# One weight load of 128 rows cut into loads of 112, 8 and 8 rows, in a decode kernel for one core

## The chip, the core and the metric

The kernel runs on one core of a Trainium2 chip. A core has five engines with queues of their own: TensorE (PE, with its weight loads shown as PEld), VectorE (DVE), ScalarE (ACT), GpSimd (POOL) and SyncE (SP), and sixteen DMA engines that move data between the chip's memory (HBM) and the core's on-chip memory (SBUF, 128 partitions). The metric is the device time of one execution, in microseconds (us).

## The reference

One step of decoding for two sequences (B = 2). Two branches take the same input x and are mixed by a gate:

```python
def reference(A_x, A_k_cache, A_v_cache, A_wq, A_wo, B_x, B_w1, B_w2, B_w3, B_w4, gate_w):
    x = A_x                                                   # [2, 1, 1024]
    g = sigmoid((x * gate_w).sum(-1, keepdims=True))
    # branch A: attention of 32 heads over a cache of 16384 positions, 128 numbers each
    q = (x @ wq).reshape(B, 1, 32, 128).transpose(0, 2, 1, 3)
    p = softmax(einsum("bhqd,bhkd->bhqk", q, k_cache) * 128 ** -0.5)
    a = einsum("bhqk,bhkd->bhqd", p, v_cache) ... @ wo
    # branch B: a mixer and an MLP
    h = gelu(layernorm(x) @ w1)
    hs = shifted_groups(h) @ w2          # each quarter of h shifted along the one position
    x1 = x + hs
    b = x1 + gelu(layernorm(x1) @ w3) @ w4      # w2: [1024, 1024], w3: [1024, 3584], w4: [3584, 1024]
    return g * a + (1 - g) * b
```

All inputs are bfloat16. With one position the four shifted groups are all zeros, so the operand of w2 is zero and hs is zero; the kernel does the product with w2 all the same, with an operand of zeros.

## The kernel before, in words

All large data passes through one buffer in SBUF, `ring`, of five slots; a slot has 32 KB in each of the 128 partitions. Every large load is one DMA issued by SP, and each partition receives one contiguous row of it. The loads come in one fixed order: the first eighth of w3, wq, w2, the rest of w3, w4, then for each of 32 pairs of heads the K cache and the V cache (two heads, two slots, 64 KB in each partition), and last wo in two halves, the second half cut into six DMAs of falling size.

The order and the waits are planned in Python before anything is emitted. `queue_load` appends a load with its slots, and `pump` (lines 306 to 317) issues the next loads as long as their slots are free; a load waits for the instruction that last read its slots. `release` gives slots back and calls `pump`. `arrived(key)` is the event on which a reader of the data waits: the semaphore of the load's last DMA and its value. Each DMA adds 16 to its semaphore, and the plan counts up by 16 for each. A load of one DMA uses the semaphore of its first slot, `s_ring`; a load of several, before, uses one semaphore for each, `s_tail`.

The slots are fixed by these lines:

```python
w_slots = {"wq": (0, 1), "w2": (2,), "w3": (3, 4), "w4": (0, 1)}
k_slots = ((2, 3), (3, 4))
```

V goes to slots 0 and 1. So wq, w2 and w3 wait for nothing, w4 waits for the matmuls with wq (L604), the first K load waits for the matmuls with w2 (L509) and for the part of w3's (L476) that reads slot 3, and each later K or V load waits for the matmuls of the pair before (L652 for K, L688 for V).

`runs` (L329) builds the DMA of a weight matrix: partition p gets rows p·r to p·r + r - 1 of the matrix in one run. For w2 that is eight rows of 1024 numbers, 16 KB in each of 128 partitions. Before, w2 is one such DMA.

In the prologue the core computes q with wq (L604), the gate (L404 to L417), the product with w2 (L509, `row_stage`), its columns (L543, L549), a layer norm, the product with w3 (L476, `dense_stage`), gelu, and the product with w4 (L509 again). Then the pairs run in a loop: DVE transposes K in place (L646), PE makes the scores (L652), a softmax over DVE, PE and ACT follows, PE multiplies with V (L688), and the result of a pair is kept. At the end come the product with wo (L727), two copies to `orow` (L756) and four small stores of the output.

ACT issues, at the start, six small loads: x and the gate weights to `xg_row`, and x in four parts to `xrow`, two rows each; and at the end two of the four stores.

## Time and profile before

| | us |
|---|---|
| median of 3 runs | 1322.31 |
| lowest run | 1322.17 |
| time of the profiled execution | 1322.18 |
| its span, first to last instruction | 1320.9 |
| PE busy in it | 786.0 (60%) |
| DVE busy in it | 659.8 (50%) |

The mean granted TensorE clock in the profiled execution is 0.794 of full speed. DMA moved 570.60 MB at a mean of 432 GB/s.

In the lines of the profile, "tile<-source" names what an instruction writes and reads, L and a number is the line of the kernel, and x and a number is how many instructions a row stands for. The slices cut the span into forty equal parts, 33.0 us each; their digits are tenths. DMA share is the mean busy share of the sixteen DMA engines. The row of a queue gives packets, megabytes and the share of the sixteen engines' span. The row of a DMA issue gives the size in KB and the time from issue to landing. The chain of waits is followed back from the last instruction; each piece has its start, its length and what ran. In a short window a DMA share can come out over 1, since packets are counted as a whole.

### The profile page before, as it was taken

To read this page: it belongs to the slowest core of one execution; us is meant where nothing else is said; L and a number is where in the kernel's file an instruction comes from. 1 tells how busy PE (TensorE), PEld (TensorE's weight loads), DVE (VectorE), ACT (ScalarE), POOL (GpSimd) and SP (SyncE) were. 2 spreads that over 40 slices of the span, in tenths; PEclk is the share of its full clock that TensorE was granted. 3 is DMA by queue.
4 is the path that set the end of the run, shared out by engine and by line. 5 is a ranking of instruction groups with operands and counts; after the bars stand their busy time and mean duration, and the time that the engine had idled before them with its cause. 6 is when DMAs were issued, how large, how long until landed. Compare 5 with 4: busy or idle time off the path is not lost.

```text
span 1320.9 us, 12282 instructions
## 1 busy us (share of the span) xinstructions
PE 786.0 (60%) x5235; PEld 335.0 (25%) x5235; DVE 659.8 (50%) x527; ACT 45.7 (3%) x99; POOL 19.6 (1%) x78
## 2 busy tenths in 40 slices
PE   1645467655546666555666655566565556756457
PEld 1622222222222222222222222222222222222223
DVE  0254446655444665544466554446655445665444
ACT  0000000000000000000000000000000000000000
POOL 3000000000000000000000000000000000000000
PEclk9976888877688877777887777788777778887778
DMA  9999999999999999999999999999999999999998
GB/s 414 433 427 441 431 431 443 431 429 443 431 429 443 431 431 441 431 433 441 429 435 439 429 435 439 431 435 437 431 435 437 431 437 435 431 439 433 431 439 370
DMA packets 11121, 570.60 MB, mean 432 GB/s; under 512 B 1235, under 2 KB 1763, under 8 KB 2022
## 3 DMA queue, kind: packets, MB, share of 16 engines
q1 hardware_dynamic: 11080, 570.43, 99.7%
q8 instruction: 8, 0.13, 0.0%
q14 instruction: 3, 0.02, 0.0%
q10 hardware_dynamic: 30, 0.01, 0.0%
HBM read 570.44 MB, written 0.00 MB: 432 GB/s over the span
## 4 chain that ended last, share of the span: by engine, by line
DMA 69%; PE 24%; DVE 6%; issue 1%; SPq 0%; POOL 0%
DMA ring<-in_A_k_cache_dram 65%; PE ps L652 22%; DVE ring L646 6%; DMA ring<-in_A_wo_dram 2%; DMA ring<-in_A_wq_dram 2%; PE ps L476 1%; PE ps L604 1%; DVE hsd L543 0%; PE ps L509 0%; PE ps L400 0%; SPq L333 0%; DVE orow L756 0%; POOL mv L441 0%; PE ps L727 0%; DVE q_f L616 0%
## 5 line engine op out<-in xcount | busy, mean ns | idle before, releaser
L652 PE MATMUL ps<-ring,Z 128*128 128x512 bf16 x2048 | 531.5, 417 | 382.3 <-DVE ring L646 381.4
L646 DVE STREAM_TRANSPOSE ring<-ring 128x2048 f32<-128x2048 f32 x256 | 565.2, 2275 | 268.2 <-DMA ring<-in_A_k_cache_dram 268.2
L652 PEld LDWEIGHTS ps<-ring,Z 128*128 128x128 bf16 x2048 | 202.3, 104 | 698.7 <-issue 457.2
L688 PE MATMUL ps<-ring,PT_sb 128*32 128x512 bf16 x2048 | 172.8, 512 | 4.2 <-DVE recip L679 4.1
L702 DVE SCALAR_TENSOR_TENSOR OT_sb<-ps,gT,recip 128x2 f32 x32 | 7.0, 219 | 208.2 <-PE ps L699 208.2
L688 PEld LDWEIGHTS ps<-ring,PT_sb 128*32 128x32 bf16 x2048 | 69.0, 124 | 94.1 <-issue 75.3
L673 ACT ACTIVATE P_sb<-ps,negm 128x512 bf16<-128x512 f32 x32 | 22.0, 687 | 998.2 <-DVE negm L671 998.2
L662 DVE TENSOR_REDUCE rA<-ps 128x1 f32<-128x512 f32 x32 | 22.1, 691 | 64.2 <-PE ps L652 64.2
L677 PE MATMUL ps<-rowsum,hsel 128*128 128x1 f32 x128 | 24.0, 292 | 38.0 <-ACT P_sb L673 38.0
L675 DVE STREAM_TRANSPOSE PT_sb<-P_sb 128x512 bf16<-128x512 bf16 x32 | 22.8, 711 | 27.0 <-ACT P_sb L673 27.0
L677 PEld LDWEIGHTS ps<-rowsum,hsel 128*128 128x128 f32 x128 | 21.3, 237 | 40.7 <-ACT P_sb L673 40.7
L664 PE MATMUL ps<-ident,rmax_bf 128*1 128x128 bf16 x32 | 7.0, 217 | 33.1 <-DVE rmax_bf L663 33.1
L634 POOL TENSOR_TENSOR Z<-q_f,mask 128x16 bf16<-128x16 f32 x32 | 8.4, 261 | 1205.9 <-PE ps L652 1205.9
L697 ACT ACTIVATE acc_sb<-ps 128x512 bf16<-128x512 f32 x32 | 19.1, 597 | 203.6 <-PE ps L688 203.6
L699 PE MATMUL ps<-dsel,acc_sb 128*128 128x2 bf16 x128 | 8.1, 167 | 22.5 <-ACT acc_sb L697 22.5
L604 PE MATMUL ps<-xT_bf,ring 128*128 128x2 bf16 x256 | 7.1, 165 | 23.2 <-DMA ring<-in_A_wq_dram 19.6
L476 PE MATMUL ps<-xn_bf,ring 128*128 128x2 bf16 x224 | 14.3, 202 | 1.4 <-DVE xn_bf L443 1.4
L699 PEld LDWEIGHTS ps<-dsel,acc_sb 128*128 128x128 bf16 x128 | 5.3, 96 | 38.3 <-ACT acc_sb L697 38.3
L664 PEld LDWEIGHTS ps<-ident,rmax_bf 128*1 128x1 bf16 x32 | 2.5, 79 | 49.0 <-DVE rmax_bf L663 49.0
L476 PEld LDWEIGHTS ps<-xn_bf,ring 128*128 128x128 bf16 x224 | 14.3, 162 | 1.4 <-issue 1.4
L665 DVE TENSOR_REDUCE m_sb<-ps 1x2 bf16<-1x128 bf16 x32 | 8.9, 279 | 9.9 <-PE ps L664 9.9
L671 DVE TENSOR_SCALAR negm<-ps,cAB 128x1 f32<-128x1 f32 x32 | 8.9, 277 | 9.3 <-PE ps L668 9.3
(98 smaller groups left out, 87.8 us busy)
## 6 DMA issues: line engine op xcount, KB each, us to landing
ring<-in_B_w_dram SPq DMA_DIRECT2D x1, 7168.0 KB, 26.3
ring<-in_B_w_dram SPq DMA_DIRECT2D x1, 6272.0 KB, 43.0
ring<-in_A_wo_dram SPq DMA_DIRECT2D x1, 4096.0 KB, 38.4
ring<-in_B_w_dram SPq DMA_DIRECT2D x1, 2048.0 KB, 28.2
ring<-in_A_wo_dram SPq DMA_DIRECT2D x1, 2048.0 KB, 22.7
ring<-in_A_wo_dram SPq DMA_DIRECT2D x1, 1024.0 KB, 24.7
ring<-in_B_w_dram SPq DMA_DIRECT2D x1, 896.0 KB, 5.5
ring<-in_A_k_cache_dram SPq DMA_DIRECT2D x32, 26.9
```

What stands on the lines that cost most here:

```text
L476: fn = lambda e, nb=nb, kl=kl: e.matmul(out_ps[:, nb, :], lhsT=cols(wv, kl, nb, nout), rhs=rhs_of(kl), start=False, stop=True, skip_group_ ...
L604: ev = pl.add("pe", lambda e, h=h, kc=kc: e.matmul(q_ps[:, h, :], lhsT=wv[:, kc, h * Dh:(h + 1) * Dh], rhs=xT_bf[:, kc, :], start=(kc == 0 ...
L646: return pl.add("dve", lambda e: e.transpose(ap, ap), waits=(arrived(("k", n)),), sig=True)
L652: ev = pl.add("pe", lambda e, bp=bp: e.matmul(S_ps[:, 0:NCOL], lhsT=Z[:, bp, ZO - 2 * u:ZO - 2 * u + P], rhs=kv[:, :, bp // 2, :, bp % 2], ...
L662: e1 = pl.add("dve", lambda e: e.tensor_reduce(rA[:, :], S_ps[:, 0:NCOL], axis=AX.X, op=ALU.max), waits=(ev_S[n],), sig=True)
L664: e3 = pl.add("pe", lambda e: e.transpose(mt_ps, rmax_bf[:, :], ident[:, :]), waits=(e2,), sig=True)
L673: e7 = pl.add("act", lambda e: e.activation(P_sb[:, :], S_ps[:, 0:NCOL], ACT.Exp, bias=negm[:, 0:1], scale=scale, accum_out=rowsum[:, 0:1] ...
L675: e8 = pl.add("dve", lambda e: e.transpose(PT_sb[:, :], P_sb[:, :]), waits=(e7,), sig=True)
L677: e9 = pl.add("pe", lambda e, hp=hp: e.matmul(l_ps[:, hp:hp + 1], lhsT=hsel[:, hp, :], rhs=rowsum[:, 0:1], start=True, stop=True, skip_gro ...
L688: ev = pl.add("pe", lambda e, jj=jj, cg=cg: e.matmul(acc_ps[32 * cg:32 * cg + 32, 0:512], lhsT=PT_sb[:, 32 * jj:32 * jj + 32], rhs=vv[:, 4 ...
L697: e1 = pl.add("act", lambda e: e.activation(acc_sb[:, :], acc_ps[:, 0:512], ACT.Copy), waits=(ev_pv,), sig=True)
L699: e2 = pl.add("pe", lambda e, w=w: e.matmul(oT_ps, lhsT=acc_sb[:, w * P:(w + 1) * P], rhs=dsel[:, w, :], start=(w == 0), stop=(w == 3)), w ...
```

## The change

w2 is loaded by three DMAs, one after the other in SP's queue: partitions 0 to 111, 112 to 119 and 120 to 127. A new function, `rows_of`, builds a DMA of some partitions of a weight matrix. All three count on the semaphore of w2's slot, which then rises by 48 in place of 16, and the readers of w2 wait for the last value. What arrives where in `ring` is the same as before, and so are all other loads and all computation.

```diff
@@ pump @@
                 for k, fn in enumerate(fns):
-                    dsem = s_ring[slots[0]] if len(fns) == 1 else s_tail[k]
+                    dsem = s_ring[slots[0]] if len(fns) == 1 or key[0] == "w2" else s_tail[k]
                     dma_done[key] = dma_done[key, k] = pl.dma("sp", (lambda e, fn=fn, idx=slots[0]: fn(e, idx)), dsem,
                                                               waits=waits if k == 0 else ())
...
+        def rows_of(Wt, width, p0, pn):
+            def fn(e, idx):
+                src = Wt.rearrange("(p r) n -> p (r n)", p=P)[p0:p0 + pn, :]
+                return e.dma_start(ring[p0:p0 + pn, idx, 0:Wt.shape[0] // P * width], src)
+            return fn
...
-        wloads[("w2", 0)] = [runs(B_w2, D, 0, NBD)]
+        PW = P - 16
+        wloads[("w2", 0)] = [rows_of(B_w2, D, p0, pn) for p0, pn in ((0, PW), (PW, 8), (PW + 8, 8))]
```

As the change is described, eight DMA engines then carry nine of w2's rows and eight carry seven, where each carried eight.

## The prediction

> **What bounds the kernel now.** I read the page's forty slices first, then its queues, the chain that ended last, the windows at both ends and last the DMA issues. The slices say that the DMA engines are busy from the first slice to the last:

> ```profile
> span 1320.9 us, 12282 instructions
> ...
> DMA  9999999999999999999999999999999999999998
> GB/s 414 433 427 441 431 431 443 431 429 443 431 429 443 431 431 441 431 433 441 429 435 439 429 435 439 431 435 437 431 435 437 431 437 435 431 439 433 431 439 370
> ...
> q1 hardware_dynamic: 11080, 570.43, 99.7%
> q8 instruction: 8, 0.13, 0.0%
> ...
> q10 hardware_dynamic: 30, 0.01, 0.0%
> ```

> The reader is to see that no slice but the last falls below nine tenths, and that one queue, SP's, moves 570.43 MB at the rate of the slices. 570.43 MB at 433 GB/s is 1317 us, nearly the whole span. So what counts is the engine that finishes last: an engine that loses a microsecond anywhere keeps that loss to the end, because it is never idle and so can never catch up. The chain of waits shows the same from the other side (start, length, what ran):

> ```profile
> 47.20 9.02 PE ps L476 x140
> 56.24 25.65 DMA ring<-in_A_k_cache_dram
> 81.92 2.32 DVE ring L646
> ...
> 84.36 8.61 PE ps L652 x32
> ...
> 92.99 27.50 DMA ring<-in_A_k_cache_dram
> ```

> A K load is 2 x 16384 x 128 numbers of two bytes, 8.39 MB; at 433 GB/s it takes 19.4 us. The one issued at 92.99 us took 27.50 us, so 27.5 - 19.4 = 8.1 us of older work stood before it; the first, issued at 56.24 us, had 25.65 - 19.4 = 6.3 us before it. The queue doesn't run dry, and compute work before those issues can be some 6 us late without an idle DMA engine.

> At the end the sixteen engines don't finish together (columns: window, its length, busy time and count for PE, PEld, DVE, ACT and POOL, granted clock, DMA share, GB/s):

> ```profile
> 10.00:20.00 10.00, 0.00 (x0) 0.00 (x0) 2.64 (x11) 1.28 (x1) 3.63 (x19) 1.00 1.00 433
> 1316.00:1317.00 1.00, 0.95 (x16) 0.39 (x16) 0.00 (x0) 0.00 (x0) 0.00 (x0) 0.57 0.97 353
> 1317.00:1317.40 0.40, 0.12 (x7) 0.10 (x8) 0.00 (x0) 0.00 (x0) 0.00 (x0) 0.50 0.70 246
> 1317.40:1317.80 0.40, 0.40 (x8) 0.00 (x0) 0.00 (x0) 0.00 (x0) 0.00 (x0) 0.50 0.58 200
> 1317.80:1318.20 0.40, 0.28 (x8) 0.09 (x4) 0.00 (x0) 0.00 (x0) 0.00 (x0) 0.50 0.36 123
> 1318.20:1318.60 0.40, 0.40 (x6) 0.08 (x2) 0.00 (x0) 0.00 (x0) 0.00 (x0) 0.50 0.02 5
> ```

> A share of 0.97, 0.70, 0.58, 0.36 is about 16, 11, 9 and 6 engines: roughly seven engines stop about a microsecond before the other nine. The chain of waits has what follows:

> ```profile
> 1292.23 25.74 DMA ring<-in_A_wo_dram
> ...
> 1318.01 0.61 PE ps L727 x4
> 1318.65 0.42 DVE orow L756
> ```

> The last weights release the last matmuls (L727), the copy (L756) and the output, so a microsecond on the latest engine is a microsecond of the time.

> **The change, part by part.** w2 is the issue of 2048.0 KB, the rest of w3 that of 6272.0 KB, with us from issue to landing last; the four small ones are all that ACT's queue 10 carries:

> ```profile
> ring<-in_B_w_dram SPq DMA_DIRECT2D x1, 6272.0 KB, 43.0
> ...
> ring<-in_B_w_dram SPq DMA_DIRECT2D x1, 2048.0 KB, 28.2
> ...
> xrow<-in_A_x_dram ACTq DMA_DIRECT2D x4, 1.0 KB
> ...
> out_dram<-orow ACTq DMA_DIRECT2D x2, 1.0 KB
> xg_row<-in_A_x_dram ACTq DMA_DIRECT2D x1, 4.0 KB
> ...
> xg_row<-in_gate_w_dram ACTq DMA_DIRECT2D x1, 2.0 KB
> ```

> SP's part of the timeline, the instructions on the ring (ns least, median, most) and the chain say when:

> ```profile
> 2.12 34.51 SPq L333 DMA_DIRECT2D ring<-in_B_w_dram  x3
> ```

> ```profile
> L333 SPq DMA_DIRECT2D ring<-in_B_w_dram x4: 328/371/543, 0.7 to 36.3; - x4
> ```

> ```profile
> 38.57 1.84 PE ps L509 x32
> ```

> *Two more issues on SP.* Each takes 0.328 to 0.543 us. Behind them on SP stands only the issue of w3; then SP waits for wq's release and issues w4 at 36.3 us. w3's packets start only when w2's are done, near 30 us, so 2 x 0.4 us of SP time near 2.1 us costs nothing; if that cover were gone it would cost 0.8 us.

> *The wait for w2.* w2 lands 28.2 us after its issue at 2.12 us, so near 30.3 us, and its first matmul runs at 38.57 us: 8 us of cover. w3, issued near 2.5 us, lands 43.0 us later, near 45.5 us, and its first matmul runs at 47.20 us: 1.7 us of cover. If w3 comes 4.8 us later, L476 starts 3.1 us later and the first K load is issued near 59.3 us; its data would start on the latest engine at 81.9 - 19.4 + 4.8 = 67.3 us. Nothing is late next.

> *The row that changes engine.* A row of w2 is 2048.0 KB / 128 = 16 KB. One engine's part of 433 GB/s is 27.1 GB/s, so a row takes 0.605 us. Before, each engine carries eight, 4.84 us. After, eight engines carry nine, +0.605 us, and eight carry seven, -0.605 us. That an eight-row load uses eight engines I take from queue 10 above: x in one load of two rows, the gate weights in one of one row, xrow in four of two rows and the output in two stores of two rows are 2 + 1 + 8 + 4 = 15 rows, and its 30 packets are 15 rows and 15 completions: one engine for each row, not sixteen for each DMA.

> *What the eight-row loads run at.* No row of the trace has a large load into few neighbouring rows of SBUF. Every large load of before covers 128 rows and runs at 433 GB/s, and this says nothing on whether the engine or its place of arrival sets the 27.1 GB/s. If places of arrival set it, sixteen of them at 27.1 GB/s make the 433, each one serving up to 128 / 16 = 8 rows, and an eight-row block of neighbours reaches few of them. With c rows to a place, each of the two small loads takes c row-times on its engines instead of one, so the eight engines need 7 + 2c row-times against eight before: c = 1 gives +1 (+0.6 us), c = 8 gives +15 (+9.1 us), c = 4 gives +7, 7 x 0.605 = +4.2 us. Between these ends I take c = 4, half of the upper one; both ends stay in the range's working. On the 112-row load, whose shares of seven no longer fall on places of eight, I put between 0 and 2 row-times of collisions and take one, +0.6 us.

> [...]

> *The sum.* From the profiled execution's own time, 1322.18 us (span 1320.9 us and 1.3 us around it): +4.2 us for two small loads at four row-times, +0.6 us for the 112-row load, 0 for SP and the waits: 1322.18 + 4.8 = **1327.0 us**. The median of the runs shown, 1322.31 us, stands 0.13 us from that execution, so I make no step between them.

> **The rivals.** *A: engines alone set the pace* (c = 1). Then only the one row counts. If the nine late engines of the last windows held all eight that are relieved, and the ninth were not loaded, the end would come 0.6 us forward: 1321.6 us. If late engines are loaded, it goes back by 0.6 us: 1322.8 us. Nine late engines and eight relieved places mean that at least one late engine gets a row more, so in this execution the gain is near nothing: 1322.4 us for the case. For a gain speaks queue 8: eight packets of 0.13 MB / 8 = 16 KB, the size of one w2 row; if each fell to another engine, eight engines are a row late, and the change could repay just them. Against: the windows' spread is nearer nine engines.

> *B: the places of arrival serve eight rows each* (c = 8): +9.1 us, with the row-time for the 112-row load +9.7 us: 1331.9 us. Every large load at one total rate allows it; nothing in the rows asks for so wide a place.

> *C: the 112-row load isn't spread over sixteen engines.* The mechanism is the split: with k engines the longest one carries 112 / k rows, 112 / k x 0.605 us against 4.84 us, and 128 rows always being a multiple of sixteen, no large load of before has tried it. It sits on w2 near 25 us. At k = 1 it is 67.8 us, +62.9 us: 1385 us, clearly slower. It decides from +26.4 us (2%), so for k of 2 or less; at k = 8 it is only +3.6 us. Against it: 112 is 7 x 16, and the one- and two-row loads of queue 10 show as many parts as rows.

> *D: the change doesn't do what it says*, the eight-row loads being cut over all sixteen engines: half a row each, 7 + 2 x 0.5 = 8 row-times as before, and with no sharing of places 1322.2 us. Queue 10's count speaks against it.

> **How the numbers follow.** The forecast (c near 4, +2.5 to +7.8 us, 1324.7 to 1330.0 us) 0.58; A 0.28; D 0.05; B 0.06; C 0.03, of which 0.02 over 2%. Changes under 2% (26 us) are about what a measurement of this kernel can't tell from none; only C passes that. Leaving out B, C, and none of the rest gives 1321.6 to 1330.0 us, which holds about 0.9; nothing narrower takes in both A and the forecast. Faster by over 2%: 0.01, since 26 us can't come from a 4.84 us load; within: 0.97; slower: 0.02.

> **What the changed profile would show.** SP's queue has 11080 packets before. With eight-row loads on eight engines it gains 16 completions, 11096; cut over sixteen engines, or with sixteen completions each, 11112 or more. Three issues of 1792.0, 128.0 and 128.0 KB replace the one of 2048.0 KB. The forecast wants a DMA share near one half over the last 4 to 5 us, where now it falls over one; A wants the fall at most 1.2 us longer or shorter than now; C a first K load tens of us late. L509 should still start near 38.6 us, L476 near 50 us by the forecast and at 47.2 us by A. I would be wrong if a few neighbouring rows arrive as fast as 128 do, or if an engine goes on with w3's rows while its small one waits.

## The result and the profile after

The changed kernel takes 1329.21 us (median of 6 runs, 1328.25 to 1329.76) against 1322.2 us before: a ratio of 1.0052, 95% interval 1.0038 to 1.0066, or +7.0 us. The forecast was 1327.0 us, +4.8 us. The profiled execution took 1329.4 us, its span is 1328.1 us. (One run of before took 1884.94 us; the comparison leaves it out.)

From the page of the changed kernel and its DMA issues (us to landing last, where the page has one):

```profile
span 1328.1 us, 12284 instructions
...
GB/s 356 409 433 431 433 438 434 430 434 438 434 430 434 438 434 430 434 438 434 430 434 438 434 428 436 436 436 428 436 436 436 428 436 436 436 428 436 436 436 356
...
q1 hardware_dynamic: 11096, 570.43, 99.7%
...
ring<-in_B_w_dram SPq DMA_DIRECT2D x1, 6272.0 KB, 49.6
...
ring<-in_B_w_dram SPq DMA_DIRECT2D x1, 1792.0 KB
...
ring<-in_B_w_dram SPq DMA_DIRECT2D x2, 128.0 KB
```

The loss stands in the first two slices. Before, they moved 414 and 433 GB/s, now 356 and 409: against 433 GB/s, 101 GB/s x 33.2 us = 3.35 MB less, 7.7 us of transfer, where before 19 GB/s x 33.0 us = 0.63 MB were missing, 1.4 us. That is 6.3 us of the 7. From the third slice on the rate is the old one. The last slice, 356 in place of 370, has about one microsecond more. SP's queue has 11096 packets, 16 more: 16 + 8 + 8 completions for w2 in place of 16.

The windows around w2 show it more closely (window, length, five engines, clock, DMA share, GB/s). The kernel before:

```profile
24.00:28.00 4.00, 2.45 (x92) 2.46 (x93) 0.00 (x0) 0.00 (x0) 0.00 (x0) 1.00 0.99 423
28.00:32.00 4.00, 3.42 (x129) 3.36 (x126) 0.00 (x0) 0.00 (x0) 0.00 (x0) 1.00 1.13 487
32.00:36.00 4.00, 0.99 (x38) 0.99 (x38) 0.00 (x0) 0.00 (x0) 0.00 (x0) 1.00 0.95 406
36.00:40.00 4.00, 2.68 (x49) 1.83 (x45) 1.62 (x9) 0.17 (x1) 0.00 (x0) 1.00 1.06 456
```

The changed kernel:

```profile
24.00:28.00 4.00, 0.51 (x19) 0.51 (x20) 0.00 (x0) 0.00 (x0) 0.00 (x0) 1.00 0.98 259
28.00:32.00 4.00, 4.00 (x156) 4.00 (x154) 0.00 (x0) 0.00 (x0) 0.00 (x0) 1.00 1.54 326
32.00:36.00 4.00, 1.36 (x51) 1.30 (x49) 0.00 (x0) 0.00 (x0) 0.00 (x0) 1.00 0.73 171
36.00:40.00 4.00, 0.00 (x0) 0.00 (x0) 0.00 (x0) 0.00 (x0) 0.00 (x0) 1.00 0.90 359
```

Over these 16 us the DMA share is 1.04 in the mean, against 1.03 before, while the rate is 279 GB/s in the mean, against 443, and 171 GB/s in one window. The engines are busy, not idle: a packet takes longer. The packets of the traces say how much longer. A trace doesn't name the load of a packet; w2's rows are told by their 16 KB and w3's by their 49 KB, and w2's are split here by the order in which they start, so that a few rows near the split may belong to the other load:

```
rows, us each                                median   mean   least to most
w2, before, all 128                           0.61    0.61   0.61 to 0.61
w2, after, the first 112 to start             1.01    0.98   0.61 to 1.36
w2, after, the last 16 (the two small loads)  1.86    1.68   1.01 to 1.99
w3, before, the 128 rows of 49 KB             1.85    1.86   1.85 to 2.36
w3, after                                     1.85    2.17   1.85 to 5.17
```

All of w2's rows together take 58.5 us longer than before, and w3's, which come next, 39.9 us longer. Over sixteen engines that is 3.7 + 2.5 = 6.2 us each, most of the +7.0 us. So two fifths of it stand in rows of w3, whose load was not changed and for which the forecast's sum has no term.

The chain of waits of the changed kernel, four pieces of it:

```profile
3.49 49.56 DMA ring<-in_B_w_dram
...
53.10 9.05 PE ps L483 x140
...
62.16 27.07 DMA ring<-in_A_k_cache_dram
```

```profile
1299.54 25.64 DMA ring<-in_A_wo_dram
```

w3 lands at 53.05 us in place of 45.5 us, 7.5 us later. Its matmuls (now L483) and the first K load follow, but that load still has 27.07 - 19.4 = 7.7 us of older work before it, so no DMA engine runs dry. The last weights land some 7 us later than before.

### The profile page after: what moved, and what is told of

It reads as the page before. It is cut to its first block, busy times and chain, and to the rows that moved or that the text cites. A ratio compares the mean times of both kernels' runs of the same rounds, so it can differ in the third digit from the quotient of the medians.

```text
span 1328.1 us, 12284 instructions
## 1 busy us (share of the span) xinstructions
PE 785.0 (59%) x5235; PEld 334.8 (25%) x5235; DVE 659.9 (50%) x527; ACT 45.7 (3%) x99; POOL 19.7 (1%) x78
## 2 busy tenths in 40 slices
DMA  9999999999999999999999999999999999999998
## 3 DMA queue, kind: packets, MB, share of 16 engines
q1 hardware_dynamic: 11096, 570.43, 99.7%
## 4 chain that ended last, share of the span: by engine, by line
DMA 70%; PE 23%; DVE 6%; issue 0%; SPq 0%
DMA ring<-in_A_k_cache_dram 65%; PE ps L659 22%; DVE ring L653 6%; DMA ring<-in_B_w_dram 4%; DMA ring<-in_A_wo_dram 2%; PE ps L483 1%; SPq L333 0%; SPq L339 0%; PE ps L734 0%; DVE orow L763 0%; SPq L86 0%
## 5 line engine op out<-in xcount | busy, mean ns | idle before, releaser
L682 DVE STREAM_TRANSPOSE PT_sb<-P_sb 128x512 bf16<-128x512 bf16 x32 | 22.8, 712 | 27.1 <-ACT P_sb L680 27.1
L671 PE MATMUL ps<-ident,rmax_bf 128*1 128x128 bf16 x32 | 6.9, 217 | 33.1 <-DVE rmax_bf L670 33.1
L483 PE MATMUL ps<-xn_bf,ring 128*128 128x2 bf16 x224 | 14.4, 202 | 1.6 <-DMA ring<-in_B_w_dram 1.6
L483 PEld LDWEIGHTS ps<-xn_bf,ring 128*128 128x128 bf16 x224 | 14.3, 172 | 1.6 <-DMA ring<-in_B_w_dram 1.6
L611 PEld LDWEIGHTS ps<-xT_bf,ring 128*128 128x128 bf16 x256 | 7.0, 104 | 29.1 <-DMA ring<-in_A_wq_dram 21.7
## 6 DMA issues: line engine op xcount, KB each, us to landing
ring<-in_B_w_dram SPq DMA_DIRECT2D x1, 6272.0 KB, 49.6
ring<-in_A_wo_dram SPq DMA_DIRECT2D x1, 2048.0 KB, 22.6
ring<-in_B_w_dram SPq DMA_DIRECT2D x1, 1792.0 KB
```

The costliest lines, as they stand in the source:

```text
L483: fn = lambda e, nb=nb, kl=kl: e.matmul(out_ps[:, nb, :], lhsT=cols(wv, kl, nb, nout), rhs=rhs_of(kl), start=False, stop=True, skip_group_ ...
L611: ev = pl.add("pe", lambda e, h=h, kc=kc: e.matmul(q_ps[:, h, :], lhsT=wv[:, kc, h * Dh:(h + 1) * Dh], rhs=xT_bf[:, kc, :], start=(kc == 0 ...
L671: e3 = pl.add("pe", lambda e: e.transpose(mt_ps, rmax_bf[:, :], ident[:, :]), waits=(e2,), sig=True)
L682: e8 = pl.add("dve", lambda e: e.transpose(PT_sb[:, :], P_sb[:, :]), waits=(e7,), sig=True)
```

## The experiments

One theory stood against three others. **P**: partitions of SBUF share paths, and rows that arrive on one path at one time divide its 27.1 GB/s (a sixteenth of 433 GB/s, 16 KB in 0.605 us); the slow packets above would be that. Against it stood **E** (only the engines' numbers of rows count), **S** (neighbouring HBM rows are slow to read) and **Q** (more DMAs on one queue and one semaphore cost the time). All runs below were timed against the kernel before; the intervals are some 0.15% (2 us) to each side, the runs of one kernel lie closer together.

### Small loads: destination, source, or engine

Each run adds eight loads of eight 16 KB rows behind the single load of w2, and nothing reads them. Over the eight, the same 64 partitions are written once. The diffs from here on are against the kernel before, but for the one with 112 and 16 rows, which is against the changed kernel. They leave out small functions that build a DMA as `rows_of` does: `extra_of(matrix, partitions, rows)` loads those rows into those partitions in the second half of w2's slot, unused at that time, and `part_of` loads a range of columns of w2 into its place.

```diff
-        wloads[("w2", 0)] = [runs(B_w2, D, 0, NBD)]
+        wloads[("w2", 0)] = [runs(B_w2, D, 0, NBD)] + [extra_of(B_w2, DST, SRC) for i in range(8)]
# neighbours:          DST = slice(8 * i, 8 * i + 8)                                  SRC = slice(64 + 8 * i, 72 + 8 * i)
# four apart:          DST = slice(32 * (i // 4) + i % 4, 32 * (i // 4) + 32, 4)      SRC as above
# neighbours, far SRC: DST as for neighbours                                          SRC = slice(i, 128, 16)
# two apart:           DST = slice(16 * (i // 2) + i % 2, 16 * (i // 2) + 16, 2)      SRC as for neighbours
# eight apart:         DST = slice(i, 64, 8)                                          SRC as for neighbours
```

**Eight neighbouring partitions.** 

> The kernel before, with eight more eight-row loads of 16 KB rows behind the one load of w2, into a part of the ring that nothing reads; load i goes to the neighbouring partitions 8i to 8i+7, so the eight cover partitions 0 to 63 once. Theory P (places of arrival: four neighbouring partitions share one path of 27.1 GB/s): each load takes 4 row-times of 0.605 us on its engines, 8 x 2.42 = +19.4 us; with the 1.9 us for a row that the trace of the changed kernel shows for its two small loads, +15 us. Rival E (an engine's own pace alone): eight rows more on eight engines, 8 x 0.605 = +4.8 us. Rival S (source: 128 KB of neighbouring HBM rows are slow to read): the same +15 to +19 us as P.

Measured 1333.08 us, ratio 1.0083 (1.0066 to 1.0099): +11.0 us. More than E's, less than P's 15 to 19; the shortfall is taken up below.

**Partitions four apart.** 

> As the run with eight neighbouring partitions, the same eight source blocks and the same 64 partitions, only grouped otherwise: load i goes to eight partitions that are four apart. Theory P: no two rows of a load share a path, one row-time each, 8 x 0.605 = +4.8 us, less what the eight engines are ahead of the others (up to 1.2 us): +3.6 to +4.8 us. Rival E: the same +3.6 to +4.8 us. Rival S: the source is as before, so +15 to +19 us.

Measured 1327.28 us, 1.0038 (1.0024 to 1.0052): +5.2 us, a little over the expected top. The same number of loads, bytes and source rows cost half as much when the rows arrive four partitions apart. Each of the 64 packets takes 0.61 us, and w3's rows behind them keep their mean of 1.86 us; in the run with neighbours these take 2.39 us in the mean.

**Neighbours, with distant source rows.** 

> As the run with eight neighbouring partitions, but each load reads eight rows of w2 that are sixteen rows (256 KB) apart in HBM. Theory P: the destination is as before, so +15 to +19 us, within 1 us of that run. Rival S: +4.8 us. Rival E: +4.8 us.

Measured 1333.77 us, 1.0086 (1.0070 to 1.0103): +11.7 us, as with neighbouring source rows. S falls.

**Two apart and eight apart.** 

> As the run with eight neighbouring partitions, but each load goes to eight partitions that are two apart, two to each group of four. Theory P with groups of four: two row-times a load, 8 x 1.21 = +9.7 us. With groups of eight: as with neighbours two blocks share, four row-times, +19.4 us. With groups of two or none: +4.8 us.

> As the run with eight neighbouring partitions, but each load goes to eight partitions that are eight apart, 0 to 56 and so on. If only neighbours share a path, one row-time a load: +4.8 us, like partitions four apart. [...]

One window shows the ladder, 34 to 40 us, while the small loads run. Four apart, two apart, eight apart, neighbours, in this order:

```profile
34.00:40.00 6.00, 3.91 (x80) 2.81 (x79) 1.62 (x9) 0.17 (x1) 0.00 (x0) 1.00 1.00 432
```

```profile
34.00:40.00 6.00, 2.24 (x48) 1.91 (x47) 1.62 (x9) 0.17 (x1) 0.00 (x0) 1.00 1.06 322
```

```profile
34.00:40.00 6.00, 1.36 (x44) 1.27 (x44) 0.22 (x1) 0.00 (x0) 0.00 (x0) 1.00 1.03 272
```

```profile
34.00:40.00 6.00, 0.00 (x0) 0.00 (x0) 0.00 (x0) 0.00 (x0) 0.00 (x0) 1.00 0.86 168
```

The share is 0.86 to 1.06 in all four, the rate falls from 432 to 168 GB/s. The share of DMA alone would have shown nothing.

### Why eight neighbours cost less than four row-times

```diff
-# neighbours:   DST = slice(8 * i, 8 * i + 8)
+# other order:  DST = slice(8 * (i // 2) + 32 * (i % 2), 8 * (i // 2) + 32 * (i % 2) + 8)
```

> As the run with eight loads to eight neighbouring partitions each, whose +11.0 us was less than the +15 to +19 us expected, with the eight loads in another order: each load to partitions 8i to 8i+7 is followed by the one 32 partitions higher, which the run with partitions eight apart has shown to use the same paths. If the +11.0 us came out low because engines got out of step and so were at different loads on different paths, two loads in a row on the same paths leave less room for it: +13 to +19 us. If a row of neighbours costs only about 2.3 row-times whatever stands behind it: +11 us again.

Measured 1339.28 us, 1.0129 (1.0114 to 1.0145): +17.1 us, with a median row of 1.96 us against 1.36 us. The same eight loads to the same partitions, in another order, cost 6 us more. So the low +11.0 us fits engines that had got out of step and stood at different loads, on different paths; when two loads in a row use the same paths that helps less. The expectation counts 32 partitions as shown by the run with eight apart, which left 32, 40, 48 and 56; of these only 32 puts two loads that share right behind one another in this order, and with it goes the rise from +11.0 to +17.1 us. In the same window:

```profile
34.00:40.00 6.00, 2.01 (x48) 1.77 (x47) 1.07 (x5) 0.00 (x0) 0.00 (x0) 1.00 1.02 135
```

### The terms of the change, one by one

**The two small loads alone**, beside the whole load of w2:

```diff
+        wloads[("w2", 0)] = [runs(B_w2, D, 0, NBD)] + [extra_of(B_w2, slice(112 + 8 * i, 120 + 8 * i), slice(112 + 8 * i, 120 + 8 * i)) for i in range(2)]
```

> The kernel before with the change's two small loads, partitions 112 to 119 and 120 to 127, 16 KB rows, behind the one load of w2, into a part of the ring that nothing reads. The price of the two small loads alone. Theory P from the 1.9 us a row of the changed kernel's trace: +3.8 us; at four row-times full +4.8 us; rival E +1.2 us. Together with the 112-row load in place of 128 rows (+8.1 us for one extra such load, less 4.84 us, +3.3 us) it should make up the change's +7.0 us.

Measured 1326.63 us, 1.0034 (1.0022 to 1.0046): +4.5 us, 2.2 us a load or 3.7 row-times, between the two prices named. The small rows themselves are only part of it: the sixteen take 27.2 us together, 3.4 us on each of eight engines, while w3's rows behind them take 36.2 us more than before (2.14 us in the mean). Over all sixteen engines the two make 4.0 us each.

**One more load of 112 rows, and one more of 128**, to partitions from 0 on (the second with 128 in place of 112):

```diff
+        wloads[("w2", 0)] = [runs(B_w2, D, 0, NBD)] + [extra_of(B_w2, slice(0, 112), slice(0, 112)) for i in range(1)]
```

> The kernel before with one more load of 112 rows of 16 KB behind that of w2, into a part of the ring that nothing reads. Theory P: seven rows on each of sixteen engines at the 1.0 us of the changed kernel's trace, +7.0 us. Rival E (engine's pace): 7 x 0.605 = +4.2 us.

> The kernel before with one more load of all 128 rows of 16 KB behind that of w2, into a part of the ring that nothing reads. Control: eight row-times on every engine, 8 x 0.605 = +4.8 us by every theory. Theory P has this load cheaper than the one of 112 rows, though it has sixteen rows more; rival E dearer by 0.6 us.

112 rows: 1330.2 us, 1.0061 (1.0045 to 1.0078), +8.1 us, a microsecond over the expectation. 128 rows: 1326.89 us, 1.0036 (1.0022 to 1.0050), +4.75 us, the expected 4.8. The two intervals just overlap, but the runs were 1330.01 to 1330.56 and 1326.87 to 1327.04. The load with sixteen rows fewer costs 3.3 us more. Its packets have a median of 0.98 us, those of the 128-row load 0.61 us. Together they take 106.8 us, 6.7 us on each engine, and w3's rows behind them 17.3 us more than before, 1.1 us on each. From 28 to 40 us, the run with 112 rows, then the run with 128:

```profile
28.00:32.00 4.00, 3.44 (x130) 3.38 (x127) 0.00 (x0) 0.00 (x0) 0.00 (x0) 1.00 1.06 315
32.00:36.00 4.00, 1.26 (x42) 1.17 (x41) 0.19 (x1) 0.00 (x0) 0.00 (x0) 1.00 1.30 351
36.00:40.00 4.00, 2.33 (x34) 1.65 (x38) 1.42 (x9) 0.17 (x1) 0.00 (x0) 1.00 0.75 284
```

```profile
28.00:32.00 4.00, 3.16 (x119) 3.10 (x117) 0.00 (x0) 0.00 (x0) 0.00 (x0) 1.00 0.97 414
32.00:36.00 4.00, 1.66 (x46) 1.41 (x45) 0.51 (x2) 0.00 (x0) 0.00 (x0) 1.00 1.27 544
36.00:40.00 4.00, 2.39 (x34) 1.41 (x34) 1.99 (x9) 0.17 (x1) 0.00 (x0) 1.00 0.98 418
```

**112 and 16 rows**, so that every engine carries eight again (7 + 1; SP's queue has 11096 packets, sixteen completions for each of the two loads):

```diff
-        wloads[("w2", 0)] = [rows_of(B_w2, D, p0, pn) for p0, pn in ((0, PW), (PW, 8), (PW + 8, 8))]
+        wloads[("w2", 0)] = [rows_of(B_w2, D, p0, pn) for p0, pn in ((0, P - 16), (P - 16, 16))]
```

> w2 in two loads, of 112 rows and of the last 16, in place of 112, 8 and 8: each of the sixteen engines carries eight rows, as in the kernel before. Theory P: the 112-row load's seven rows take the 1.0 us each that the trace of the changed kernel shows (7 x 0.4 = +2.8 us), and the 16 rows arrive at four paths, four to a path, 3 x 0.605 = +1.8 us: +4.6 us. Rival I (the uneven number of rows is the cost): 0. If it comes out near the changed kernel's +7.0 us, the uneven rows cost nothing beyond the sharing.

Measured 1327.44 us, 1.0040 (1.0025 to 1.0054): +5.3 us. With even numbers of rows most of the cost is still there, so uneven rows aren't the main cause. With the 112-row load at 8.1 - 4.8 = +3.3 us, the 16 rows cost 2.0 us in one row on each engine, 3.3 row-times, where groups of four neighbours would make it four.

### Three DMAs, and uneven rows, without the sharing

```diff
-        wloads[("w2", 0)] = [runs(B_w2, D, 0, NBD)]
+        wloads[("w2", 0)] = [part_of(B_w2, c0, c1) for c0, c1 in ((0, 7168), (7168, 7680), (7680, 8192))]
```

> w2 in three loads of all 128 rows each, of 14, 1 and 1 KB a row: as many DMAs, issues and semaphore steps as the change, and the engines' rows even and their places apart. Theory P: 0 to +0.1 us. Rival Q (the two more DMAs on one queue and their shared semaphore are the cost): +7.0 us, as the change.

Measured 1322.22 us, 1.0001 (0.9992 to 1.0010). Three DMAs in place of one, on one semaphore, cost nothing that can be measured (the kernel before took 1322.15 us beside it). Q falls.

In the next run, whose diff shows the new lines alone, `part_of` is given the partitions too:

```diff
+        wloads[("w2", 0)] = [part_of(B_w2, slice(0, P), 0, 7168)] + [
+            part_of(B_w2, slice(b + j, b + 32, 4), 7168, 8192) for b in range(0, P, 32) for j in range(4)]
```

> The aim of the change without its sharing: w2 as one load of 128 rows of 14 KB and sixteen eight-row loads of 2 KB rows, each to eight partitions that are four apart. Eight engines carry 8 x 14 + 16 x 2 = 144 KB, nine rows' worth, and eight carry 112 KB, seven rows' worth, as the change means it. If the late engines are those that are relieved: -0.6 us and less, by some 0.2 us for sixteen more completions. If a late engine is among the eight that are loaded, which the +5.2 us of the eight loads four partitions apart (against +4.8 us of the 128-row control) speaks for: +0.6 to +1.0 us. Theory P with the sharing as the whole cost: in any case under +1.2 us, against +7.0 us for the change.

Measured 1324.54 us, 1.0017 (1.0008 to 1.0026): +2.4 us. It is 4.6 us better than the change and worse than the kernel before. It also misses its own +1.2 us. Half of its small loads go to the upper 64 partitions, and here w3's rows are slowed: 1.96 us in the mean and 3.13 us at most, against 1.86 and 2.36 us in the kernel before, and 1.86 us in the run whose small loads went four apart into the lower 64 alone. So this run isn't free of sharing. That is 13.1 us in all, 0.8 us on each of sixteen engines; how the rest splits between the row more on eight engines and their sixteen more completions (0.009 us each in the median of the kernel before, 0.14 us together) wasn't separated. Uneven rows with little sharing didn't make the kernel faster, and no run here beats the kernel before.

## Why the prediction was right, and which term was off

- **The mechanism held, but reached further than forecast.** The price comes from what the forecast named: rows that share a place of arrival, not the rows that change engine, not SP, not the semaphore. The forecast charged it to w2's rows alone; 2.5 of the 6.2 us found in the packets stand in w3's rows. The rate is the old one after the second slice, and what was lost stays lost to the end.
- **The two small loads** were put at four row-times each, 4.84 us together; alone they cost +4.5 us. The number is near, the way to it is only in part the forecast's: their own rows take 3.4 us on eight engines, and the slowed rows of w3 make up most of the rest. The choice of c = 4 was a middle between 1 and 8 that no row of before gave, so that it hit is partly luck; the runs with partitions two and four apart, at +10.2 and +5.2 us, fit the four. That both small loads fall on the same eight engines, as the sum has it, no run shows by itself; in the changed kernel eight of w3's rows start at 30.6 to 31.2 us and the next not before 33.1 us, which fits eight engines held up by both.
- **The 112-row load was the mis-sized term.** It was put at eight row-times, 4.84 us, with one row-time of collisions; one extra such load costs 8.1 us, 13.4 row-times. That is +3.3 us on the sum. By the measured parts the change is -4.75 + 8.1 + 4.5 = +7.9 us, and it measured +7.0 us; the 0.9 us between them lie within the intervals. I had counted collisions as if only a few rows met; in the changed kernel the median row took 1.01 us, and 109 of the first 112 took over 0.7 us, so nearly every row met another. Which engine carries which of the 112 rows no run shows, and so why it is 1.65 row-times and not more or less stays open.
- **Rivals.** A (+0.6 us at most) falls with the 1.0 to 2.0 us rows. B falls with the run four apart. C and D fall with the packets: 11096 in the changed kernel, 16 + 8 + 8 completions; 11208 with one more load of 112 rows, which is 112 rows and 16 completions more; and 11112 with the two small loads beside w2, 16 rows and 16 completions more.
- **What the changed profile would show.** Packets and issues came as said. The DMA share at the end did not fall to one half for 4 to 5 us:

```profile
1320.00:1322.00 2.00, 1.47 (x48) 0.77 (x40) 0.00 (x0) 0.00 (x0) 0.00 (x0) 1.00 1.00 409
1322.00:1323.00 1.00, 0.00 (x0) 0.00 (x0) 0.00 (x0) 0.00 (x0) 0.00 (x0) 1.00 0.92 340
1323.00:1324.00 1.00, 0.71 (x16) 0.30 (x16) 0.00 (x0) 0.00 (x0) 0.00 (x0) 0.77 0.67 238
1324.00:1325.00 1.00, 0.57 (x12) 0.10 (x8) 0.00 (x0) 0.00 (x0) 0.00 (x0) 0.50 0.18 64
1325.00:1326.00 1.00, 0.92 (x12) 0.25 (x8) 0.14 (x1) 0.00 (x0) 0.00 (x0) 0.50 0.04 12
```

  A share of 0.18 is three engines, 0.04 less than one: most engines end together, a few trail by a microsecond or two. The step that failed is that only the eight engines with small rows would be late. Of the first 112 rows 109 are slow, at seven to an engine too many for half of the engines to be spared. The small loads make the others late too: in the run with the two of them alone, +4.5 us, the share from 1319.2 us on is 1.00, 0.91, 0.42 and 0.07 in four windows of 1 us, so there too no eight engines end 4 us ahead. The slowed rows of w3 fit that.
- **L509** (now L516) was to start near 38.6 us and started at 44.19 us, and the w3 matmuls at 53.10 in place of 50 us. The second is the larger delay of w3. The first I had not seen at all: see the last section. Both stay under the cover worked out for the first K load.

## What to carry to other kernels

The full 128-row load of w2 kept its rows apart, all at 0.61 us; with rows cut off it to even out engines, rows met on one path (a median of 1.01 us in the 112-row load, 1.86 us in the small ones), and the cut cost 7.0 us where the evening out could give 0.6 us. The load behind it paid too: w3's rows took 2.17 us in the mean in place of 1.86. When a transfer is to be split, split it along the columns and keep all 128 partitions in each part: that cost nothing here (1322.22 us against 1322.15). Read GB/s beside the DMA share: in the 16 us around w2 the share was 1.04 at 279 GB/s in the changed kernel and 1.03 at 443 GB/s before; a row that took 1.86 us in place of 0.61 counts as busy all that time.

## What the runs showed of the hardware that I had not expected

A load of 112 rows takes longer than one of 128: 8.1 us against 4.75 us for one more of each at 16 KB a row.

PE's stop in the middle of the wq matmuls grew. The timeline before, and after (start, length, and in brackets the idle time before):

```profile
35.01 1.16 PE L604 MATMUL ps<-xT_bf,ring 128*128 128x2 bf16 x38 [3.59 <-issue]
```

```profile
40.70 1.26 PE L611 MATMUL ps<-xT_bf,ring 128*128 128x2 bf16 x42 [7.34 <-issue]
...
44.19 1.23 PE L516 MATMUL ps<-ring,shT_bf 128*2 128x256 bf16 x18
```

No semaphore that the profile shows ends this stop, of 3.59 us before and 7.34 us after. In the traces the first 16 KB packet of queue 8, the queue of instruction packets, starts at 32.56 us before and at 38.14 us after, and PE goes on 2.4 and 2.6 us after those starts. In the traces of all fourteen kernels the packet starts at 31.4 to 38.1 us, and PE goes on 2.3 to 3.1 us after it. That the stop is PE waiting for its own instructions, which stand behind slow rows on a DMA engine, is my estimate from these times and was not tried alone. It costs nothing at the end, since the first K load has its cover, but a kernel that is bound by PE there could lose some 3.7 us more to it.
